# Residuals and means added on VectorE, output blocks turned one layer later, and weight sums stored in whole rows, in a fused routing attention and MLP kernel

## The chip, the cores and the metric

The kernel runs on one core of one Trainium2 chip. The metric is the device time of one execution in microseconds (us). A core has five engines with a queue each: TensorE (PE: matmuls, with weight loads, PEld, beside them), VectorE (DVE), ScalarE (ACT), GpSimd (POOL) and SyncE (SP). Each works through its instructions in order; semaphores tie them together. DMA transfers are issued from SP, ACT or POOL. Here only POOL issues transfers that add to what lies at the destination.

## The reference

```python
# q, k, v: (4, 8, 768, 64), centroids: (8, 16, 64), fp32; w_ch1: (512, 2048), w_ch2: (2048, 512)
mask = q_assign[:, :, :, None] == k_assign[:, :, None, :]     # the same nearest centroid
scores = np.where(mask, scale * np.matmul(q, k.transpose(0, 1, 3, 2)), -1e9)
attn = softmax(scores)
x = np.matmul(attn, v).transpose(0, 2, 1, 3).reshape(4, 768, 512)
xn = (x - mu) / np.sqrt(var + 1e-06) * g_ln                   # mean and variance over the 512
out = x + np.maximum(xn @ w_ch1, 0.0) @ w_ch2                 # fp32
```

## The kernel before, in words

**Stages.** The attention of all four batches comes first: 16 pairs of heads, each in turn. Its results go to DRAM twice, features by positions (`xT_d[b]`) and positions by features (`x_d[b]`). While it runs, the two weight matrices are loaded in chunks (`raw`) and converted; POOL finishes each chunk by a transfer that adds its second half (`w<-tb`, L274). Then come, for batch 0, a first and a second layer, and for batches 1, 2 and 3 each a first layer and a deep layer.

**The first layer** is x times w1 with seven instead of eight products for each pair of 2x2 blocks. It has eight units `j`, each with seven parts (`first_layer(b, j, part)`); parts 4 and 3 of a unit are issued inside the next one. A part is four matmuls with 384 columns (L810). VectorE adds the results (L841), ScalarE copies banks (L836) and applies ReLU (L849). `w1_sums` prepares block sums of w1 on VectorE for the next unit. `unit_end` is the work behind a unit: rows for the next batch's statistics (`norm_rows`), in batch 1 the splitting of w2 (`w2_split`), block sums of the hidden values (`outer_sums`), and from unit 5 on the first loads of the ring.

**The deep layer** is hidden times w2 with two levels of the scheme: seven outer products `m` in the order 4, 7, 1, 6, 5, 2, 3, each made of seven inner ones `way`, so 49 steps (`STEPS`), written here as (m, way). Ways 4 and 3 of a product come behind way 2 of the next. A step (`deep_product`) is four pairs of matmul records with 192 columns (L1084); its weights are a quarter of a block of w2, 256 KB, loaded into a ring of ten slots (`ring_load`), ten steps ahead, on SP. Its hidden operand is a quarter or a sum of quarters: `inner_sums` (L1058, L1060) and `inner_late` (L1065, L1067) make the sums on VectorE. Results are drained by `put_in`: copies by ScalarE (L1097) where nothing is added, additions by VectorE (L1099) where an earlier block is added. After each step `behind(m, way)` puts other work into the queues:

- the last two parts of the first layer and `outer_sums` of its last units at (4, 2), `outer_late` at several steps (L1046);
- `add_rest`: the residual, by accumulating transfers on POOL (L1123), eight per layer;
- `norm_load`, `norm_stats`, `norm_stat_rows`, `norm_center`, `norm_apply`: the next batch's rows are loaded, the mean is added by four accumulating transfers on POOL (L583), the scale is applied by VectorE (L593);
- `sum_onto` (L1164), and one accumulating transfer of block 7 onto block 4 (`m<-m`, L1204);
- `x_sum`, `w1_sums`: sums for the next first layer;
- `turn` (L1135): VectorE transposes a finished output block in 32x32 pieces, and `leave` stores it in eight transfers of 48 KB (L1147), two per step on SP. In the last batch the block of product 3 goes out in four parts (`last_part`, L1173).

**Order and queues.** In the first and deep layers of batches 1 to 3 the orders of TensorE, VectorE, ScalarE and SP are those of the program text. In the attention and in batch 0 SP's order is chosen by the scheduler when the kernel is built. Buffers rotate in pools: `unit` has eight of 128x768, `row` two (rows of statistics), `sums` two.

**Stored weights.** `w2_all` is a copy of w2 in DRAM, stored in four transfers of 1 MB in batch 1's first layer; `w2_t` holds four sums of blocks, `w2_d` the sums of quarters. A ring load from `w2_d` reads 2 KB in a row for each partition, one from `w2_all` or `w2_t` reads four pieces of 512 B.

Of the kernel before, what the change touches and what calls it, by code (L numbers as in the profile page):

```python
# [19 lines left out]
def kernel(  # L20
# [528 lines left out]
    def norm_stats(b, parts=range(2)):  # L549
# [9 lines left out]
        if 1 in parts:  # L559
            stat = moments[b, "stat"]  # L560
            if b == 0:
                nc.vector.tensor_scalar_mul(stat[:, 0, :], mv[:, :, 1], -1.0)
            else:
                nc.vector.tensor_copy(stat[:, 0, :], mv[:, :, 0 if b == 1 else 1])
            nc.vector.reciprocal(stat[:, 1, :], stat[:, 1, :])

    def norm_stat_rows(b):
# [7 lines left out]
        for i in range(2):  # L575
            if i or b < 2:
                row = xpool.tile([P, S], F32, tag="row", name="stat_row", bufs=2)
                nc.sync.dma_start(out=row, in_=stat_d[b][i : i + 1, :].to_broadcast([P, S]))
                moments[b, i] = row

    def norm_center(b):
        for c in range(NDC):
            nc.gpsimd.dma_start(  # L583
                out=normed[b][0][:, c, :], in_=stat_d[b][0:1, :].to_broadcast([P, S]), accum_op=ALU.add
            )
# [299 lines left out]

    def w2_sum(st, i):
        if i in (1, 3):
            st["t", i] = xpool.tile([P, NFH, MH], F32, tag="sums", name=f"w2t{i}", bufs=2)
        elif i == 2:
            st["t", 2] = xpool.tile([P, NFH, MH], F32, tag="sums", name="w2t2", bufs=2)  # L890
        o, x, y = {
            1: lambda: (st["t", 1], w2_block(0, 1), w2_block(0, 0)),
            2: lambda: (st["t", 2], w2_block(1, 1), st["t", 1]),
            3: lambda: (st["t", 3], w2_block(1, 1), w2_block(0, 1)),
            4: lambda: (st["t", 2], w2_block(1, 0), st["t", 2]),
        }[i]()
        for c in range(0, NFH, 2):
            nc.vector.tensor_tensor(o[:, c : c + 2], x[:, c : c + 2], y[:, c : c + 2], ALU.subtract)
# [13 lines left out]
    def second_product(bank, tt, lhs, rhs, first):  # L912
        for c in range(NFH):
            nc.tensor.matmul(  # L914
                bank[:, :MH], hidden[lhs + (c,)][:, tt * P : (tt + 1) * P], rhs[:, c, :],
# [24 lines left out]
    def second_layer(b, tt, part, st):  # L940
        if part == 1:
            st["x", tt] = ps("x_ps")
            second_product(st["x", tt], tt, (0, 0), w2_block(0, 0), True)
            st["p1", tt] = add_rows(b, 0, tt, 0, st["x", tt])
        elif part == 2:
            y = ps("y_ps")
            second_product(y, tt, (0, 1), w2_block(1, 0), True)
# [14 lines left out]
        elif part == 3:  # L962
            second_product(st["z", tt], tt, (0, 1), w2_block(1, 1), False)
# [18 lines left out]
    w2_all = spill.tile([NFC, P, DM], F32, name="w2_all")  # L982
# [3 lines left out]
    def w2_keep(i, t):  # L986

        nc.sync.dma_start(out=w2_t[i - 1], in_=t.rearrange("p c f -> p (c f)"))

    def w2_back(i):  # L990
        t = splits.tile([P, NFH, MH], F32, tag="t", name="w2_t")
        nc.sync.dma_start(out=t.rearrange("p c f -> p (c f)"), in_=w2_t[i - 1])
        return t

    def w2_split(m, src):

        blocks = [[src[:, l * NQH : (l + 1) * NQH, j * P : (j + 1) * P] for j in range(2)] for l in range(2)]
# [9 lines left out]
    def w2_operand(m, way):  # L1007
# [3 lines left out]
        if m in SUMS:  # L1011
            src = w2_t[SUMS.index(m)].rearrange("p (c f) -> p c f", f=MH)
        else:
            r, k = {1: (0, 0), 2: (1, 0), 3: (1, 1)}[m]
            src = w2_all[r * NFH : (r + 1) * NFH, :, k * MH : (k + 1) * MH].rearrange("c p f -> p c f")
        return src[:, l * NQH : (l + 1) * NQH, j * P : (j + 1) * P]
# [31 lines left out]
    def inner_sums(st, m, which):  # L1048

        (a11, a12), (a21, a22) = quarters(m)  # L1050
        if 0 in which:
            if "tmp" not in st:
                st["tmp"] = xpool.tile([P, 3, S], F32, tag="sums", name="qs", bufs=2)
                st["n"] = 0
# [3 lines left out]
            nc.vector.tensor_tensor(s1, a21, a22, ALU.add)  # L1058
# [534 lines left out]
```

## Time and profile before

| what | value |
|---|---|
| median of 3 runs | 936.92 us (936.36 to 942.41) |
| the profiled execution | 935.08 us, span 933.2 us, mean clock 0.984 |
| busy | PE 890.0, PEld 582.4, DVE 683.6, ACT 392.7, POOL 121.1 us |
| DMA | 151.39 MB, mean 162 GB/s; queue q1 (SP) 52.3%, q0 (POOL) 16.2% of 16 engines' span |
| first layer of batch 1, deep layer of batch 1 | 475.0 to 544.4, 544.4 to 629.5 us |
| first layer of batch 2, deep layer of batch 2 | 629.5 to 699.2, 699.2 to 778.3 us |
| first layer of batch 3, deep layer of batch 3 | 778.3 to 847.9, 847.9 to 917.7 us |

A line of the windows view gives a stretch, its length, the busy time of each engine with its number of instructions, the granted TensorE clock (PEclk, 1.00 is full), the mean busy share of the 16 DMA engines and their GB/s. A share a little over 1 comes from transfers that reach over the edge of a stretch. A line of the chain view gives start, length and what the chain of latest releases went through; "DMA m<-xT_d" is a transfer to `m` from `xT_d`. In a timeline the bracket at the end is the idle time ahead of the instruction and what ended it. In the DMA view the last number is the median time from issue to landing.

### The profile page before, as it was taken

What the parts mean: (1) busy time and instruction counts of PE and PEld (TensorE: products, weight loads), DVE (VectorE), ACT (ScalarE), POOL (GpSimd) and SP (SyncE); (2) the same over time, 40 slices, a digit from 0 to 9 for tenths busy, and PEclk for the clock granted to TensorE, in tenths of its full rate; (3) what the DMA queues carried; (4) which work ended last, traced back from release to release, by engine and by line L of the source; (5) the groups of instructions that cost most, each with busy time, mean ns of one, the idle gap of its engine ahead of it and who ended that gap; (6) DMA issues with size and microseconds to landing.
All of it is one profiled execution on the core that took longest, in us unless ns stands there. A gap on an engine that the chain in (4) does not pass through costs nothing.

```text
span 933.2 us, 13290 instructions
## 1 busy us (share of the span) xinstructions
PE 890.0 (95%) x4724; PEld 582.4 (62%) x4724; DVE 683.6 (73%) x1145; ACT 392.7 (42%) x715; POOL 121.1 (13%) x178
## 2 busy tenths in 40 slices
PE   8999999999999999999999988989999799999993
PEld 4444444444444455588865568975558796557992
DVE  6999999998988878985647667664548586447672
ACT  4777768999767723310025521004551001332100
POOL 1122222211212111100000003210002120000220
PEclk9999999999999999999999999899999899999997
DMA  7788899896994457644347779972137996102994
GB/s 155 161 174 159 182 179 199 193 230 130 205 176 96 101 138 172 172 146 155 123 141 283 266 263 211 285 134 58 32 115 196 257 229 138 37 1 67 235 215 80
DMA packets 286440, 151.39 MB, mean 162 GB/s; under 512 B 211856, under 2 KB 251392, under 8 KB 285344
## 3 DMA queue, kind: packets, MB, share of 16 engines
q1 hardware_dynamic: 253728, 125.61, 52.3%
q0 software_dynamic: 28176, 24.13, 16.2%
q10 hardware_dynamic: 4464, 0.74, 0.4%
q8 instruction: 39, 0.64, 0.3%
q14 instruction: 33, 0.27, 0.1%
HBM read 107.61 MB, written 33.25 MB: 151 GB/s over the span
## 4 chain that ended last, share of the span: by engine, by line
PE 55%; DMA 6%; issue 2%; DVE 2%; POOL 0%; SPq 0%; DVEq 0%; POOLq 0%
PE x_ps L810 18%; PE z_ps L810 9%; PE x_ps L1084 8%; PE x_ps L914 4%; PE y_ps L810 4%; PE z_ps L1084 4%; DMA m<-xT_d 2%; PE z_ps L914 2%; DMA w<-w_all 2%; PE y_ps L1084 2%; DMA m<-m 1%; PE y_ps L914 1%; PE s_ps L386 1%; PE a_ps L398 1%; DMA out_dram<-y 1%
## 5 line engine op out<-in xcount | busy, mean ns | idle before, releaser
L381 ACT ACTIVATE e<-s_ps 128x768 f32<-128x768 f32 x192 | 151.7, 812 | 9.1 <-PE s_ps L386 4.9
L386 PE MATMUL s_ps<-t,t 64*128 64x384 f32 x768 | 154.9, 483 | 0.0
L398 PE MATMUL a_ps<-e,v_sb 128*64 128x384 f32 x768 | 130.9, 490 | 0.0
L398 PEld LDWEIGHTS a_ps<-e,v_sb 128*64 128x64 f32 x768 | 52.3, 137 | 75.8 <-issue 62.8
L1084 PE MATMUL x_ps<-lower,w 128*128 128x192 f32 x448 | 84.5, 336 | 12.6 <-issue 5.6
L841 DVE TENSOR_TENSOR lower<-z_ps,u 128x384 f32<-128x384 f32 x56 | 31.1, 556 | 81.7 <-PE z_ps L810 54.6
L386 PEld LDWEIGHTS s_ps<-t,t 64*128 64x128 f32 x768 | 68.2, 188 | 35.1 <-issue 34.2
L1123 POOL DMA_DIRECT2D m<-xT_d x24 | 32.6, 1461 | 440.8 <-ACT m L1097 198.7
L1084 PEld LDWEIGHTS x_ps<-lower,w 128*128 128x128 f32 x448 | 76.0, 195 | 16.9 <-issue 9.3
L836 ACT COPY p<-x_ps 128x384 f32<-128x384 f32 x32 | 15.1, 472 | 137.5 <-PE x_ps L810 137.5
L386 PE MATMUL s_ps<-mask,mask 64*128 64x384 bf16 x384 | 63.0, 324 | 1.1 <-ACT e L381 0.7
L849 ACT ACTIVATE lower<-lower 128x384 f32<-128x384 f32 x88 | 45.2, 522 | 41.8 <-DVE lower L841 41.8
L433 DVE TENSOR_TENSOR two<-e 128x1536 f32<-128x1536 f32 x30 | 52.6, 1753 | 12.6 <-ACT e L381 12.3
L836 ACT COPY u<-x_ps 128x384 f32<-128x384 f32 x64 | 30.7, 479 | 69.8 <-PE x_ps L810 69.8
L436 DVE TENSOR_TENSOR two<-two,e 128x1536 f32<-128x1536 f32 x30 | 52.5, 1750 | 1.7
L810 PE MATMUL x_ps<-xn,w 128*128 128x384 f32 x128 | 46.6, 487 | 0.0
L810 PE MATMUL x_ps<-xn,ws 128*128 128x384 f32 x128 | 46.5, 486 | 0.0
L810 PE MATMUL z_ps<-xn,ws 128*128 128x384 f32 x128 | 46.5, 486 | 0.0
L810 PE MATMUL x_ps<-xt,w 128*128 128x384 f32 x128 | 46.5, 486 | 0.0
L810 PE MATMUL z_ps<-xt,ws 128*128 128x384 f32 x128 | 46.5, 486 | 0.0
L810 PE MATMUL y_ps<-xn,w 128*128 128x384 f32 x128 | 46.5, 486 | 0.0
L810 PE MATMUL x_ps<-xt,ws 128*128 128x384 f32 x128 | 46.5, 486 | 0.0
(212 smaller groups left out, 1499.2 us busy)
## 6 DMA issues: line engine op xcount, KB each, us to landing
w<-w_d SPq DMA_DIRECT2D x84, 256.0 KB, 5.2
raw<-in_moe_w_ch_dram SPq DMA_DIRECT2D x32, 512.0 KB, 4.9
w<-w_t SPq DMA_DIRECT2D x36, 256.0 KB, 6.1
w<-tb POOLq DMA_DIRECT2D x32, 256.0 KB, 6.4
w_d<-wt SPq DMA_DIRECT2D x7, 1024.0 KB, 5.5
w<-w_all SPq DMA_DIRECT2D x27, 256.0 KB, 5.9
v_sb<-in_v_dram SPq DMA_DIRECT2D x32, 192.0 KB, 5.9
xr<-x_d SPq DMA_DIRECT2D x24, 256.0 KB, 3.0
```

The costliest lines, as they stand in the source:

```text
L381: nc.scalar.activation(e, s[:, :, :HC], AF.Exp, scale=SCALE)
L386: nc.tensor.matmul(s[:, j, :HC], of_keys[:, keys], of_queries[:, o : o + HC], start=part == first, stop=part != first, skip_group_check=True,)
L398: nc.tensor.matmul(acc[j * D : (j + 1) * D, :HC], loaded[n]["v"][:, j, c, :], e[:, j, :], start=(c == 0), stop=(c == NT - 1),)
L433: nc.vector.tensor_tensor(two, soft.pop(u), soft.pop(u + 1), ALU.add)
L436: nc.vector.tensor_tensor(two, two, soft.pop(u + 2), ALU.add)
L810: nc.tensor.matmul(bank[:, :HC], lhs[:, c, :], rhs[:, c], start=first and c == 0, stop=c == NDH - 1, skip_group_check=True,)
L836: nc.scalar.copy(t, bank[:, :HC])
L841: nc.vector.tensor_tensor(h, bank[:, :HC], other, ALU.add)
L849: nc.scalar.activation(h, h, AF.Relu)
L914: nc.tensor.matmul(bank[:, :MH], hidden[lhs + (c,)][:, tt * P : (tt + 1) * P], rhs[:, c, :], start=first and c == 0, stop=c == NFH - 1, sk ...
L1084: nc.tensor.matmul(bank, w[:, c, :], a[:, c], start=way in (1, 2, 5) and c == 0, stop=c == NQH - 1, skip_group_check=True,)
L1123: nc.gpsimd.dma_start(out=o[:, h].rearrange("p (t q) -> p t q", t=NT), in_=xT_d[b][2 * j + h].rearrange("p (t q) -> p t q", t=NT)[:, :, r ...
```

## The change

- The residual is loaded into SBUF by two plain transfers per layer on SP (`rest_load`) and added by VectorE (`add_rest`), four times per layer. The mean is subtracted by VectorE (`norm_apply` with `i` = 0), four times. Block 7 is added to block 4 by VectorE. Products 6 and 5 no longer add an earlier block as their banks are drained; whole blocks are added later (`sum_onto`, five per layer, before two).
- Of the four output blocks of batches 1 and 2, one is turned in the deep layer; three are turned behind units 0 and 1 of the next first layer, from a list `pending`, and stored four transfers per unit. The turned blocks lie in the `row` buffers; `unit` has six buffers. In the last batch all are turned earlier, and SP and ACT share the stores.
- `outer_sums`, three quarters of the first `inner_sums`, `norm_stats` and `norm_stat_rows` move from the deep layer into the first layer, parts 4 and 3 of its last unit to (4, 1) and (4, 2).
- `w2_all` and `w2_t` are laid out by quarters, so that every ring load reads 2 KB in a row. `w2_all` is stored in 16 transfers, which the scheduler places on SP in the attention and in batch 0's first and second layer. Split 6 of w2 moves from unit 7 to unit 6.

```diff
     def norm_stat_rows(b):
...
         for i in range(2):
-            if i or b < 2:
-                row = xpool.tile([P, S], F32, tag="row", name="stat_row", bufs=2)
-                nc.sync.dma_start(out=row, in_=stat_d[b][i : i + 1, :].to_broadcast([P, S]))
-                moments[b, i] = row
-
-    def norm_center(b):
-        for c in range(NDC):
-            nc.gpsimd.dma_start(
-                out=normed[b][0][:, c, :], in_=stat_d[b][0:1, :].to_broadcast([P, S]), accum_op=ALU.add
-            )
+            row = xpool.tile([P, S], F32, tag="row", name="stat_row", bufs=2)
+            nc.sync.dma_start(out=row, in_=stat_d[b][i : i + 1, :].to_broadcast([P, S]))
+            moments[b, i] = row
...
-    w2_all = spill.tile([NFC, P, DM], F32, name="w2_all")
+    w2_all = spill.tile([2, 2, 2, 2, P, NQH * P], F32, name="w2_all")
...
+    def w2_whole(back):
+        for r in range(2):
+            for k in range(2):
+                for l in range(2):
+                    for h in range(2):
+                        c, m = r * NFH + l * NQH, k * MH + h * P
+                        w = w2[:, c : c + NQH, m : m + P]
+                        d = w2_all[r, k, l, h].rearrange("p (c f) -> p c f", f=P)
+                        nc.sync.dma_start(out=w if back else d, in_=d if back else w)
...
     def unit(name):
-        return units.tile([P, 2, HC], F32, tag="unit", name=name, bufs=8)
+        return units.tile([P, 2, HC], F32, tag="unit", name=name, bufs=6)
...
-    def add_rest(b, r, j, o):
-        for h in range(2):
-            nc.gpsimd.dma_start(
-                out=o[:, h].rearrange("p (t q) -> p t q", t=NT),
-                in_=xT_d[b][2 * j + h].rearrange("p (t q) -> p t q", t=NT)[
-                    :, :, r * 2 * Q : (r + 1) * 2 * Q
-                ],
-                accum_op=ALU.add,
-            )
+    def rest_load(b, k):
+        if b + 1 == B and k:
+            t = xpool.tile([P, 3, S], F32, tag="sums", name="rest_x", bufs=2)[:, :2]
+        else:
+            t = units.tile([P, 2, S], F32, tag="rest", name="rest_x", bufs=1)
+        nc.sync.dma_start(out=t, in_=xT_d[b][2 * k : 2 * k + 2].rearrange("h p s -> p h s"))
+        rest_x[b, k] = t
+
+    def add_rest(b, r, k, o):
+        o = o.rearrange("p h (t q) -> p h t q", t=NT)
+        x = rest_x[b, k].rearrange("p h (t q) -> p h t q", t=NT)[:, :, :, r * 2 * Q : (r + 1) * 2 * Q]
+        nc.vector.tensor_tensor(o, o, x, ALU.add)
...
-    def turn(b, r, j, o):
-        y = unit("y")
+    def turn(b, r, k, o):
+        y = xpool.tile([P, S], F32, tag="row", name="y", bufs=2)
...
-            onto = {6: 1, 5: 6, 2: 1, 3: 5}.get(m)
+            onto = {2: 1, 3: 5}.get(m)
...
+        def between():
+            first_layer(b, NFH - 1, 3)
+            relu(len(summed))
+            outer_sums(NFH - 1, True)
+            rest_load(b, 0)
+            if more:
+                norm_load(b + 1)
+            else:
+                rest_load(b, 1)
...
+        jobs = {
+            (4, 1): [lambda: first_layer(b, NFH - 1, 4)],
+            (4, 2): [between],
+            (4, 3): [rest(1, 0, 4)],
+            (7, 6): [s4(0)], (7, 4): [s4(1)], (7, 3): [s4(2)], (1, 6): [s4(3)],
+            (1, 4): [onto(4, 7)], (6, 3): [onto(6, 1)],
+            (5, 4): [onto(4, 6)], (5, 3): [onto(5, 6)], (2, 6): [onto(7, 5)],
+        }
...
+        if more:
+            for at, (i, c) in (
+                ((4, 4), (0, 0)), ((7, 5), (0, 1)), ((1, 3), (0, 2)), ((6, 6), (0, 3)),
+                ((6, 5), (1, 0)), ((6, 4), (1, 1)), ((5, 6), (1, 2)), ((5, 5), (1, 3)),
+            ):
+                jobs.setdefault(at, []).append(norm(i, c))
+            jobs[2, 4] = [out_of(1, 0, 4)]
+            jobs[2, 3] = [rest(0, 0, 2), lambda: rest_load(b, 1)]
+            jobs[3, 6] = [lambda: x_sum(b + 1, 1)]
+            jobs[3, 5] = [lambda: w1_sums(b + 1, 0, (0, 1))]
+            jobs[3, 4] = [lambda: x_sum(b + 1, 2)]
+            later(
+                rest(1, 1, 7), out_of(1, 1, 7), out_of(0, 0, 2), None,
+                rest(0, 1, 3), out_of(0, 1, 3), None,
+            )
+        else:
+            jobs[1, 3] = [rest(1, 1, 7)]
+            jobs[5, 6] = [rest(0, 0, 1), onto(4, 6)]
+            del jobs[5, 4]
+            jobs[2, 5].append(rest(0, 1, 5))
+            jobs[2, 1] = [out_of(1, 0, 4)]
+            jobs[2, 7].append(out_of(1, 1, 7))
+            jobs[2, 3] = [out_of(0, 0, 2)]
...
-            leave(2)
+            leave(2 if more else 4, (nc.sync,) if more else (nc.sync, nc.scalar))
...
+            if part == 5 and b and j:
+                outer_sums(j - 1, b > 1 or j > 4)
+                if j + 1 == NFH:
+                    inner_sums(deep[b], ORDER[0], cs=slice(0, NQH - 1))
...
-                m = (1, 5, 3, 4, 2, 7, None, 6)[j]
+                m = (1, 5, 3, 4, 2, 7, 6, None)[j]
...
-            if j > 1:
-                outer_sums(j - 2, b > 1)
+                if j in (5, 6):
+                    outer_late("s", "e", (0, 0), j - 5)
+            while pending:
+                job = pending.pop(0)
+                if job is None:
+                    break
+                job()
+            if b + 1 < B and j + 2 == NFH:
+                norm_stats(b + 1)
+            if b + 1 < B and j + 1 == NFH:
+                norm_stat_rows(b + 1)
+            leave(4)
```

## The prediction

> **What bounds the kernel now.** I read the busy shares first (TensorE, "PE", 890.0 of 933.2 us), then cut the span into stages at the places where TensorE changes from the first layer (L810) to the deep layer (L1084). These are the stretches of the windows view; the columns are length, busy PE, weight loads, DVE (VectorE), ACT (ScalarE), POOL (GpSimd), clock, DMA share, GB/s.
>
> ```profile
> 544.40:629.50 85.10, 72.83 (x402) 69.28 (x401) 61.37 (x101) 5.96 (x18) 14.94 (x13) 0.94 0.95 216
> 699.20:778.30 79.10, 70.84 (x403) 67.46 (x402) 57.12 (x96) 6.08 (x18) 14.98 (x13) 0.96 0.96 212
> 847.90:917.70 69.80, 67.20 (x401) 64.95 (x399) 51.23 (x87) 5.74 (x16) 13.08 (x11) 1.00 0.88 191
> 917.70:933.20 15.50, 0.04 (x1) 0.00 (x0) 0.74 (x2) 0.00 (x0) 0.00 (x0) 0.57 0.23 38
> 629.50:699.20 69.70, 69.70 (x219) 41.08 (x218) 32.71 (x69) 33.52 (x82) 0.00 (x0) 1.00 0.25 69
> 778.30:847.90 69.60, 69.60 (x217) 41.00 (x216) 32.71 (x69) 24.39 (x52) 0.00 (x0) 1.00 0.17 47
> ```
>
> The same deep layer takes 85.1, 79.1 and 69.8 us in batches 1, 2 and 3; behind it comes a tail of 15.5 us without matmuls. The first layers between (the last two lines) are full for TensorE, and there DVE is busy for 47% and DMA for 17 to 25%. A deep step (eight matmul records) takes 1.30 us in the timeline, a first-layer part 1.29, so TensorE's floor for 49 steps and two parts is 66.3 us. The losses are 18.8, 12.8, 3.5 and the tail. The chain of waits names what fills them:
>
> ```profile
> 576.65 10.76 DMA m<-m
> ...
> 598.66 9.52 DMA m<-xT_d
> ...
> 613.32 6.52 DMA m<-xT_d
> ...
> 721.21 17.79 DMA w<-w_all
> ```
>
> First the accumulating POOL transfers that add residuals (`m<-xT_d`) and blocks (`m<-m`), then weight quarters for the ring (`w<-`). TensorE's own timeline shows the second kind:
>
> ```profile
> 577.38 1.46 PE L1084 MATMUL x_ps<-w 128*128 128x192 f32 x8
> 583.06 2.93 PE L1084 MATMUL y_ps<-w 128*128 128x192 f32 x8 [4.22 <-DMA w<-w_t]
> 585.78 2.89 PE L1084 MATMUL x_ps<-lower,w 128*128 128x192 f32 x8
> ```
>
> The weights were late by 4.22 us, and the next two steps ran at twice their time; that is the 0.94 in the clock column. Why late: the DMA view of 721 to 740 us.
>
> ```profile
> q0 software_dynamic: 2012, 2.29, 72.2%
> ...
> w<-w_d SPq DMA_DIRECT2D x6, 256.0 KB, 7.9
> w<-w_t SPq DMA_DIRECT2D x3, 256.0 KB, 12.5
> ```
>
> POOL's queue takes 72% of the engines for 2.29 MB, and weights land in 8 to 12.5 us; at 700 to 712 us, without it, they land in 2.6 and 3.5. The ring covers ten steps, 13 us.
>
> **The change, part by part.**
>
> *POOL's additions leave (batches 1 to 3).* Per layer go 8 `m<-xT_d` (192 KB), 4 `xn<-stat_d` (384 KB, 15.1 us each to land; batches 1, 2) and one `m<-m`. In come two plain loads `rest_x` of 768 KB. DMA demand of a middle layer: 39 ring loads of 256 KB, 10.2 MB; next rows 1.6; `rest_x` 1.6; stores 0.4: 13.8 MB in 66.3 us, 208 GB/s. From 531 to 544 us the trace shows 323 GB/s on plain loads and stores alone. The tightest stretch is the start, where 3.1 MB of rows and residuals come beside the ring: at 323 GB/s a ring load is 9.7 us later, plus 2.6 to land, 12.3 against 13 us of cover. Much of it is issued gradually, so I cost it at nothing; without the cover it costs 1 to 3 us in batches 1 and 2 each.
>
> *VectorE takes them.* Wide operations (128x768; 0.95 us, but issued every 0.87 us in a row, 571.42 to 572.29) in a deep layer of batch 2: before 14+14 inner sums, 4 outer, 4 scalings, 2 block sums, 4 turns, 2 row sums = 44. After: 12+14, 4, 4 scalings and 4 centerings, 5 block sums, 2 residuals, 1 turn, 2 row sums = 48. Reads of a bank (0.36 us, every 0.27): 37 before, 29 after, as products 6 and 5 no longer add an earlier block and their copies go to ACT, 0.32 us each, which is busy for 6 of 79 us. So 48x0.87+29x0.27 = 49.6 us against 48.3: about equal, but in 66 instead of 79 us. The new list gives nearly every step of 1.30 us one wide operation and at most one read (1.14 us); exceptions (two wide ones at steps 5 of products 7, 6, 5) are followed by lighter steps. DVE also waited 3.52 us at 608.28 and 3.36 at 619.93 for `m<-xT_d`; with it went TensorE's waits on `lower L1065` (1.25, 1.09). Next late is the copy `u3` between the last products: 0.45 us stays, as in batch 3.
>
> *Outer sums and the first inner sums move into the first layer.* Each deep layer now starts with 3.60, 2.00 and 2.01 us without matmuls ahead of (4,6): DVE ends L1065 at 553.3, TensorE starts at 553.41. After, DVE has only two short sums (0.3 us each) and L1065 left after the last first-layer add: 1.0+0.5+0.6+1.0 = 3.1 us after the layer's start, and (4,6) is due at 2x1.30+2x1.29 = 5.2. These stalls go. Batch 1's units 5 and 6 get fuller: 3 adds and 4 weight sums (3.2), outer 1.5, splitting 2.6, `outer_late` 0.9 = 8.2 of 9.03 us. The split of sum 6 comes a unit earlier, 9 us after its load is issued; the 1 MB load lands in 7.4. Hidden; else it delays DVE by 1 to 2 us, which unit 7 (no splitting) takes up.
>
> *Whole rows.* 21 ring loads per layer come in 2 KB instead of 512 B rows. The row: 3.5 us for `w_t` in 512 B pieces against 2.6 for `w_d` in 2 KB, in the same quiet 12 us. The Trainium skill, "DMA: Bandwidth & Descriptors", Specifications, says that transfers reach line rate from 512 B on, so this part would bring nothing. By the row it saves 21x0.9 = 19 us of landing per layer, by the rule 0; on TensorE's path both make 0 once POOL's traffic is gone, since either lies within 13 us. I take the row for the cover alone. The 16 stores of `w2_all` move ahead to the attention and batch 0's first layer, in SP's queue before `raw` loads: the first group waits for a weight's addition issued at 352.10 (landing in 6.4: 358.5; next `raw` 361.2), the second to about 381 (next `raw` 381.67). Hidden by 2.7 and 0.7 us; bounds 0 to +6. I take +0.5.
>
> *Three blocks turned later.* Per batch 24 of 32 stores move into the next first layer, four per unit on SP (0.62 us each to issue, 2.8 to land). DVE gets 2 residuals and 3 turns there, 4.5 us in two units with half their time free. **It adds a wait:** the fourth turn reuses the buffer of the second, whose last four stores are issued only in unit 1, in batch 2 behind a row load that waits for ACT's statistics. By durations DVE arrives 17 us after the layer's start, the statistics end at 17.6, four issues 20.5, landing 23.3: DVE stands 6 us. Queued behind it are the adds of unit 2, and the weight sums that unit 3's part 6 needs at 6.45+9.03+9.03+3x1.29 = 28.4 (five, seven, seven and three parts); DVE, with the turn (0.9), two adds (1.0) and the sums (1.5) to do, has them at 26.7. Hidden by 1.7 us; bounds 0 and +5. I take +1.0.
>
> *The tail.* After the last matmul SP is still issuing a backlog:
>
> ```profile
> 921.30 2.41 SPq L1147 DMA_DIRECT2D out_dram<-y  x3
> 923.81 3.85 SPq L1177 DMA_DIRECT2D out_dram<-y  x6
> ```
>
> The last turn ends at 918.55; SP's last issue at 927.66; 5.5 us lie behind it. After, the first two blocks are turned at products (2,1) and (2,7) and SP and ACT share the stores. Of ACT's work only one copy, (5,4), lies behind two of them. What is left is four short stores, two per queue, 1.3 us, and some lag: 0.8+1.3+5.5+0.9 = 8.5 instead of 15.5.
>
> **The sum.** Deep layers to the floor plus 0.75 for the last copies and 1.0 for small lateness of DVE: 68.0, 68.0; batch 3 without row work 67.2. Gains 17.1+11.1+2.6+7.0 = 37.8; costs 0.5+1.0. Net -36.3 from the profiled run's 935.08 (span 933.2 plus 1.9): 898.8, **899 us**. The median of the runs shown, 936.92, is 1.8 higher, well inside the range.
>
> **Rivals.**
> *VectorE becomes the bound.* It would have 75% of the deep layer by issue times, in order, so each wait for ACT or a load is passed on. Against it: batch 3 does 43 us of this work in 69.8 and hardly delays TensorE. Then all three layers stay at 69.8: -15.3-9.3-0, tail -4, first layers +3: 909.5.
> *The ring stays late.* For it: 12.3 against 13 us above. Half of the losses of batches 1 and 2 stay: -15.8, batch 3 -1, tail -3: 915.
> *The stores hold DVE, and the time rises.* The place is unit 1 of batches 2 and 3. TensorE is safe for 7.8 us of DVE's standing (6.1 plus the 1.7 left). Beyond that each us costs one, in two layers; the 37.8 us are used up when the wait reaches 27 us, and at 29 the time is 935.1-37.8+0.5+42.4 = 940. Against it: 24 stores behind the deep layer of batch 1 took 23.33 us of SP (0.97 each), so four take 4.
>
> **How the numbers follow.** Forecast 0.63, VectorE 0.19, late ring 0.10, stores 0.05, better than all costs 0.03. The floors without any cost give 935.1-35.1-7.9 = 892. The range 892 to 917 reaches over the late ring. A measurement of this kernel can tell about 1% from no change: faster by more than that (below 927.6) takes the first three and the last, less some for causes unseen, 0.91; within 1% 0.04; slower 0.05.
>
> **What would show it.** Right: deep layers of 67 to 69 us at a DMA share near 0.7 and clock 1.00; no q0 traffic behind 410 us; ring loads landing in 3 to 5 us; TensorE back to back at (4,6); a tail near 8.5. Wrong: first layers of batches 2 and 3 longer than 69.7 with DVE's turn waiting for `out_dram` (stores); PE waits on `w<-` (ring) or on DVE's L1074 and L1108 lines (VectorE); holes before 400 us with DVE waiting for `raw`.

## The result and the profile after

The changed kernel takes **897.56 us** (median of 4 runs, 896.93 to 900.04) beside 939.26 us (4 runs of the kernel before, 936.36 to 942.41). The ratio is 0.956, with a 95% interval from 0.9517 to 0.9603. The forecast was 899, the range 892 to 917. The profiled execution took 897.76 us, with a span of 896.0.

The windows view, cut at the same places as before. The columns are stretch, length, busy PE, PEld, DVE, ACT and POOL with their numbers of instructions, clock, DMA share, GB/s. The lines are the deep layers of batches 1, 2 and 3, then the tail, then the first layers of batches 2 and 3.

```profile
544.00:614.00 70.00, 67.01 (x402) 65.06 (x401) 58.04 (x89) 8.32 (x25) 0.00 (x0) 1.00 0.75 234
683.70:750.80 67.10, 66.65 (x402) 65.28 (x401) 57.53 (x88) 8.31 (x25) 0.00 (x0) 1.00 0.72 225
820.40:887.50 67.10, 66.65 (x401) 65.06 (x399) 52.47 (x84) 8.17 (x24) 0.00 (x0) 1.00 0.72 197
887.50:896.00 8.50, 0.15 (x1) 0.00 (x0) 0.73 (x2) 0.00 (x0) 0.00 (x0) 0.74 0.23 38
614.00:683.70 69.70, 69.70 (x218) 40.97 (x217) 39.12 (x84) 33.76 (x83) 0.00 (x0) 1.00 0.29 71
750.80:820.40 69.60, 69.60 (x218) 41.05 (x217) 38.94 (x82) 24.39 (x52) 0.00 (x0) 1.00 0.23 56
```

The deep layers went from 85.1, 79.1 and 69.8 us to 70.0, 67.1 and 67.1, at full clock, and the tail from 15.5 to 8.5. The first layers took the three turns and stayed at 69.7. POOL does nothing any more in these stages. The page's DMA issues (number, KB each, median us to landing) show the ring in time:

```profile
w<-w_d SPq DMA_DIRECT2D x84, 256.0 KB, 3.4
w<-w_t SPq DMA_DIRECT2D x36, 256.0 KB, 4.9
w<-w_all SPq DMA_DIRECT2D x27, 256.0 KB, 3.2
```

TensorE's timeline shows the start of the deep layer of batch 1. In the kernel before, (4,6) began 3.60 us late, and the steps behind it took up to 2.77 us:

```profile
548.35 1.45 PE L810 MATMUL z_ps<-xn,ws 128*128 128x384 f32 x4
553.41 1.68 PE L1084 MATMUL x_ps<-lower,w 128*128 128x192 f32 x8 [3.60 <-issue]
554.88 2.77 PE L1084 MATMUL z_ps<-qs,w 128*128 128x192 f32 x8
```

In the changed kernel it is back to back; the last line is the one loss that is new:

```profile
547.91 1.45 PE L803 MATMUL z_ps<-xn,ws 128*128 128x384 f32 x4
549.35 1.54 PE L1093 MATMUL x_ps<-lower,w 128*128 128x192 f32 x8
...
565.13 1.57 PE L1093 MATMUL x_ps<-lower,w 128*128 128x192 f32 x8 [2.54 <-DMA w<-w_all]
```

Where it comes from is seen on SP (same kernel, timeline of SP's queue; the length is that of the issues):

```profile
544.76 0.36 SPq L574 DMA_DIRECT2D stat_d<-st  x1
549.08 0.80 SPq L577 DMA_DIRECT2D stat_row<-stat_d  x2
...
551.94 0.44 SPq L1137 DMA_DIRECT2D rest_x<-xT_d  x1
552.43 3.42 SPq L521 DMA_DIRECT2D xn<-xT_d  x4
556.30 1.46 SPq L1035 DMA_DIRECT2D w<-w_all  x2
```

SP stands from 545.1 to 549.1 for the store of the statistics, because it has to load them back. Then the residual and four row blocks, 2.3 MB, go out in one piece, and the ring load stands behind them. In batch 2 the same list of issues costs nothing; there SP stands for the store for only 1.0 us:

```profile
684.56 0.32 SPq L574 DMA_DIRECT2D stat_d<-st  x1
685.85 0.80 SPq L577 DMA_DIRECT2D stat_row<-stat_d  x2
```

The difference lies ahead of the store: in batch 1 SP had issued 1 MB of split weights (`w_d<-wt`) and four ring loads from 540.8 to 544.5, and the DMA engines were full until 548; in batch 2 it had issued nothing from 676 us on.

### The profile page after: what moved, and what is told of

Read it like the earlier page. It is cut to its first block, busy times and chain, and to the rows that moved or that the text cites. A ratio compares the mean times of both kernels' runs of the same rounds, so it can differ in the third digit from the quotient of the medians.

```text
span 896.0 us, 13278 instructions
## 1 busy us (share of the span) xinstructions
PE 879.3 (98%) x4724; PEld 576.4 (64%) x4724; DVE 701.6 (78%) x1158; ACT 400.1 (45%) x739; POOL 77.9 (9%) x141
## 4 chain that ended last, share of the span: by engine, by line
PE 62%; DMA 2%; DVE 0%; SPq 0%; issue 0%; ACT 0%
PE x_ps L803 18%; PE x_ps L1093 11%; PE z_ps L803 9%; PE z_ps L1093 6%; PE x_ps L910 5%; PE y_ps L803 5%; PE y_ps L1093 3%; PE z_ps L910 2%; PE y_ps L910 1%; PE s_ps L386 1%; DMA w<-w_all 1%; PE a_ps L398 1%; DMA w<-w_d 1%; DMA stat_d<-st 0%; PE den_ps L452 0%; DVE u L1108 0%
## 5 line engine op out<-in xcount | busy, mean ns | idle before, releaser
L1093 PE MATMUL x_ps<-lower,w 128*128 128x192 f32 x448 | 81.2, 327 | 3.4 <-DMA w<-w_all 2.5
L1093 PEld LDWEIGHTS x_ps<-lower,w 128*128 128x128 f32 x448 | 73.9, 190 | 5.7 <-DMA w<-w_all 2.8
L386 PEld LDWEIGHTS <-mask 64*128 64x128 bf16 x384 | 19.2, 94 | 42.3 <-issue 11.3
```

The source lines that it names most:

```text
L386: nc.tensor.matmul(s[:, j, :HC], of_keys[:, keys], of_queries[:, o : o + HC], start=part == first, stop=part != first, skip_group_check=True,)
L1093: nc.tensor.matmul(bank, w[:, c, :], a[:, c], start=way in (1, 2, 5) and c == 0, stop=c == NQH - 1, skip_group_check=True,)
```

## The experiments

Twelve more kernels ran. To compare them I cut each trace at the same places. All lengths are us of one profiled execution each; "start" is where the deep layer of batch 1 begins, "deep 1" to "deep 3" are the deep layers of batches 1 to 3. The times are medians. The kernels ran in three groups, each on a chip of its own, on which the kernel before had 937.3, 938.6 and 939.1 us; the ratios given are to these. A difference of 1 to 2 us between the times of two groups says little; the lengths of the stages say more.

| kernel | time | start | deep 1 | deep 2 | deep 3 | tail |
|---|---|---|---|---|---|---|
| before | 939.3 | 544.5 | 85.1 | 79.1 | 69.8 | 15.5 |
| before, whole rows alone | 936.9 | 544.5 | 84.1 | 80.4 | 71.5 | 14.3 |
| the same, nobody waits for the residual | 928.4 | 543.5 | 78.1 | 82.3 | 71.1 | 13.8 |
| only the order, residual at its old places | 918.8 | 544.2 | 77.4 | 72.7 | 73.6 | 8.8 |
| only the order | 909.3 | 543.5 | 75.2 | 69.9 | 71.7 | 8.0 |
| after, residual and mean by POOL | 907.4 | 544.1 | 72.9 | 69.0 | 71.6 | 8.2 |
| after, mean by POOL | 900.9 | 544.9 | 71.6 | 68.9 | 67.2 | 7.9 |
| after, residual by POOL | 900.2 | 544.1 | 68.1 | 67.0 | 71.6 | 7.9 |
| after, 512 B pieces | 900.0 | 544.0 | 72.2 | 67.1 | 67.2 | 8.2 |
| after, sums back in the deep layer | 904.2 | 543.6 | 70.8 | 70.8 | 69.4 | 8.5 |
| after, all turns in the deep layer, slow stores at the end | 914.7 | 543.9 | 74.3 | 68.9 | 67.2 | 17.5 |
| after, more work for VectorE | 900.5 | 544.1 | 69.7 | 67.1 | 68.5 | 8.3 |
| after, loads spread out | 896.0 | 544.4 | 67.0 | 67.0 | 67.2 | 9.4 |
| after | 897.6 | 544.0 | 70.0 | 67.0 | 67.2 | 8.3 |

### 1. Whole rows, taken away and alone

```diff
-    w2_all = spill.tile([2, 2, 2, 2, P, NQH * P], F32, name="w2_all")
+    w2_all = spill.tile([NFC, P, DM], F32, name="w2_all")
...
+                if j < 4:
+                    cs = slice(j * NFC // 4, (j + 1) * NFC // 4)
+                    nc.sync.dma_start(out=w2_all[cs].rearrange("c p f -> p c f"), in_=w2[:, cs])
```

> The changed kernel with the old layout of w2_all and w2_t (ring loads from them read 512 B pieces) and w2_all stored in batch 1's first layer again. Theory (the accumulating transfers of POOL were the disturbance, short pieces cost only landing time inside the ring's cover): 897 to 900 us, at most 2 us above the changed kernel, all of it at the start of the deep layer of batch 1, where a ring load was late by 2.54 us already. Rival (whole rows bring a good part of the gain): 908 us or more, with waits on w<-w_t and w<-w_all in all three deep layers.

Measured: 899.95 us (899.43 to 900.07; ratio 0.9579, 0.9549 to 0.9608). The loss lies in batch 1's deep layer, 72.2 instead of 70.0; the late ring load is the same one, now with a wait of 3.12 us. Only 0.6 us of the loss is the longer wait; the rest is that the next two steps took 2.52 and 2.24 us, at a granted clock near 0.6. So whole rows are worth about 2 us in this execution, and only where the ring is at its limit. By the times alone it is not certain: one of the four runs of the changed kernel, 900.04 us, was as slow as these.

The other way round, the kernel before with this layout alone:

> The kernel before with the layout by quarters alone (whole rows of 2 KB, w2_all stored in 16 transfers early); the POOL transfers stay. Theory: 934 to 939 us, the waits on w<- in batches 1 and 2 stay, as POOL's queue still holds 72% of the engines at the ring's loads. Rival (whole rows bring a good part): 920 to 928 us, the waits of 4.22 and 17.79 us on w<-w_t and w<-w_all mostly gone.

Measured: 936.88 us (10 runs, 935.31 to 939.23; ratio 0.9989, 0.9971 to 1.0007). No gain that can be measured, and the time is the one that the theory expected. The trace is not: the waits for `w<-`, which were to stay, went. First the waits of TensorE and VectorE in the kernel before, from the waits view (total, times, longest; us); VectorE's from 540 us on:

```profile
PE y_ps L1084 <- DMA w<-w_t: 5.7, 2, 4.2
...
PE x_ps L1084 <- DVE lower L1065: 2.3, 2, 1.3
...
DVE p L1099 <- DMA m<-xT_d: 11.9, 4, 3.5
```

The same rows with whole rows alone:

```profile
PE x_ps L1098 <- DVE lower L1079: 12.4, 3, 6.9
...
PE y_ps L1098 <- DMA w<-w_t: 0.2, 1, 0.2
...
DVE p L1113 <- DMA m<-xT_d: 22.9, 5, 9.1
```

The ring was repaired: TensorE's waits for `w<-` fell from 9.0 us (5.7, 2.0 and 1.3) to 1.3 (0.9, 0.2 and 0.2). The time stayed, since a second wait had been lying underneath. VectorE, draining products 2 and 3 (`p<-x_ps,m`), adds a block onto which POOL is still adding the residual. With the ring on time TensorE arrives earlier, VectorE stands longer, and TensorE stands for VectorE.

### 2. Residual and mean, one by one and together

```diff
     def add_rest(b, r, k, o):
-        nc.vector.tensor_tensor(o, o, x, ALU.add)
+        for h in range(2):
+            nc.gpsimd.dma_start(out=o[:, h]..., in_=xT_d[b][2 * k + h]..., accum_op=ALU.add)
```

("..." inside a line stands for what is left out of it. The plain loads of `rest_load` are not issued either.)

> The changed kernel, but the residual is again added by POOL's accumulating transfers (eight of 192 KB per layer) at the places where VectorE adds it now. Theory: half of the POOL traffic is back, 1.57 MB per layer in all three layers; 903 to 912 us, ring loads landing later, and VectorE standing for m<-xT_d in front of the turn that follows. Rival (what brought the gain is the moved sums and the later turns, and VectorE has no room): 897 to 899 us or a little faster, since VectorE gives up four wide operations per layer.

Measured: 900.17 us (900.01 to 900.36; ratio 0.9583, 0.9554 to 0.9613). That lies between the theory's 903 to 912 and the rival's 897 to 899. In batch 2 nothing is lost (67.0), and batch 1 even gains 1.9 (68.1): without the plain load of the residual at its start the late ring load is late by 0.9 us and not 2.54. All of the loss is in batch 3 (71.6 instead of 67.2), the one batch where the new list adds the residual onto block 1 at (5,6), a few steps before the drain of product 2 reads that block. The timelines of VectorE and, below, of TensorE in batch 3:

```profile
869.58 0.36 DVE L1108 TENSOR_TENSOR p<-x_ps,m 128x192 f32<-128x192 f32 x1 [3.60 <-PE z_ps L1093]
...
881.01 0.36 DVE L1108 TENSOR_TENSOR p<-x_ps,m 128x192 f32<-128x192 f32 x1 [1.90 <-DMA m<-xT_d]
```

```profile
870.86 1.57 PE L1093 MATMUL x_ps<-lower,w 128*128 128x192 f32 x8 [1.29 <-DVE lower L1074]
...
882.29 1.57 PE L1093 MATMUL x_ps<-lower,w 128*128 128x192 f32 x8 [0.51 <-DVE lower L1074]
```

The first bracket names a matmul on `z_ps`, but the drain reads `x_ps` and `m`, and POOL had issued its two transfers to `m` at 862.55, which land in a median of 6.0 us in this stretch: of several waits the row names one, and here the transfer is the one that fits.

The mean alone:

```diff
                 norm_load(b + 1)
+                norm_center(b + 1)
...
-                ((4, 4), (0, 0)), ((7, 5), (0, 1)), ((1, 3), (0, 2)), ((6, 6), (0, 3)),
```

`norm_center` is four transfers of 384 KB that add the mean, on POOL.

> The changed kernel, but the mean is again added by four accumulating transfers of 384 KB on POOL, issued right behind the loads of the next rows, in batches 1 and 2 only. Theory: these fall on the tightest stretch, 3 to 18 us behind the start of the deep layer; the ring is late by 3 to 8 us in each of the two layers, 904 to 914 us, batch 3 unchanged at 67.1. Rival (the gain is from the moved sums and later turns): 897 to 899 us.

Measured: 900.94 us (900.72 to 901.55; ratio 0.959, 0.956 to 0.9619): 1.6 and 1.9 us in the deep layers of batches 1 and 2, as ring waits of 0.6 to 1.1 us each. The mechanism is the expected one, the size is below the expected 3 to 8.

Both together:

> The changed kernel with residual and mean both added by POOL's accumulating transfers again; whole rows, moved sums and later turns stay. Alone the residual cost 2.6 us and the mean 3.4. Theory A (contention: the transfers together starve the ring, as the prediction had it): much more than the sum, 915 to 925 us, with ring waits of 10 us and more in each of the deep layers of batches 1 and 2. Theory B (the transfers hurt before because a drain on VectorE waited for them, which the new order of additions has taken away): about the sum, 902 to 907 us.

Measured: 907.36 us (905.71 to 908.05; ratio 0.9676, 0.9634 to 0.9717), 9.8 above the changed kernel, where the two alone make 6.0. The excess is in batch 1. POOL issues the first residual among the mean's four transfers, its second half behind all four, at about 562 us; it lands some 20 us later, and VectorE's block sum waits for it:

```profile
585.48 0.96 DVE L1186 TENSOR_TENSOR m<-m,m 128x768 f32<-128x768 f32 x1 [9.83 <-DMA m<-xT_d]
```

Contention (theory A) would have given 915 or more; the order (theory B), 902 to 907, is nearer.

### 3. The order alone

The changed kernel with three of its contents undone: residual and mean by POOL, 512 B pieces, the old time of storing. What stays is where and when everything is done: the sums moved into the first layer, the later turns, the list of additions, the two queues for the last stores. Block 7 onto block 4 stays with VectorE too.

> The changed kernel with all three transfers' parts undone: residual and mean by POOL, weights in 512 B pieces, w2_all stored in batch 1's first layer. What is left of the change is the order: sums moved into the first layer, whole blocks added later, three blocks turned later, stores on two queues in the last batch. Theory A (contention): the ring is late as in the kernel before, 918 to 928 us. Theory B (order): 904 to 911 us, since pieces alone cost 2.4 us and the two additions alone 2.6 and 3.4.

Measured: 909.30 us (907.68 to 911.93; ratio 0.9702, 0.9657 to 0.9747). Its deep layers and tail in the windows view:

```profile
543.50:618.70 75.20, 69.64 (x402) 66.68 (x401) 52.99 (x83) 8.34 (x25) 11.88 (x11) 0.98 0.94 229
688.50:758.40 69.90, 67.57 (x403) 65.10 (x402) 52.33 (x82) 8.34 (x25) 11.90 (x11) 1.00 0.95 228
828.00:899.70 71.70, 67.83 (x401) 64.95 (x399) 49.01 (x79) 8.19 (x24) 10.61 (x8) 1.00 0.86 185
899.70:907.70 8.00, 0.00 (x0) 0.00 (x0) 0.74 (x2) 0.00 (x0) 0.00 (x0) 0.77 0.21 37
```

POOL's transfers are all there but one (`m<-m`) and the DMA share is 0.94 and 0.95, as before the change. Yet the deep layers of batches 1 and 2 take 145.1 us together and not 164.2. **Of the 27 us gained in these two stages, 19 come from the order, with block 7's addition, and 8 from what else VectorE and the layout took over.** The ring is a part of the 8: TensorE waits for `w<-` for 6.9 us in this kernel, 9.0 before and 2.5 after the change. Batch 3 gains nothing from the order (71.7, before 69.8).

Is it the waiting for transfers, or the moved sums and turns? The same kernel, with POOL's residual put back to where it was issued before:

```diff
-            (4, 3): [rest(1, 0, 4)],
+            (7, 6): [s4(0), rest(1, 0, 4)],
-            (1, 4): [onto(4, 7)], (6, 3): [onto(6, 1)],
+            (1, 4): [onto(4, 7), rest(1, 1, 7)], (6, 3): [onto(6, 1), rest(0, 0, 1)],
-            (5, 4): [onto(4, 6)], (5, 3): [onto(5, 6)], (2, 6): [onto(7, 5)],
+            (5, 4): [onto(4, 6)], (5, 3): [onto(5, 6), onto(7, 5), rest(0, 1, 5)],
```

In batch 3 of this kernel block 4 is turned before block 6 is added to it, so that part of the sum is missing there; the instructions are the same in number.

> The kernel with only the order of the change (909.3 us measured: residual and mean by POOL, 512 B pieces), with POOL's residual transfers put back to where the kernel before issued them: onto block 4 at (7,6), onto 7 at (1,4), onto 1 at (6,3) and onto 5 at (5,3), whose blocks the drains of products 2 and 3 add soon after. Theory B (what held the kernel before was a drain or a block sum on VectorE that waits for a transfer): 915 to 925 us, VectorE waiting for m<-xT_d in each deep layer and TensorE for VectorE behind it. Rival (it was the moved sums and the later turns): 908 to 911 us.

Measured: 918.78 us (915.69 to 920.29; ratio 0.9774, 0.9735 to 0.9812), 9.5 above "only the order". Each deep layer is longer by 1.9 to 2.8 us, in batch 3 with the same eight transfers of residuals in it, and VectorE stands as the expectation said; from its timeline, batches 1, 2 and 3:

```profile
601.95 0.36 DVE L1105 TENSOR_TENSOR p<-x_ps,m 128x192 f32<-128x192 f32 x1 [2.67 <-DMA m<-xT_d]
...
744.46 0.36 DVE L1105 TENSOR_TENSOR p<-x_ps,m 128x192 f32<-128x192 f32 x1 [3.07 <-DMA m<-xT_d]
...
885.05 0.36 DVE L1105 TENSOR_TENSOR p<-x_ps,m 128x192 f32<-128x192 f32 x1 [3.97 <-DMA m<-xT_d]
```

So the waits for the residual are 5.0 of the 19 us in batches 1 and 2. Undone one by one in the changed kernel (experiments 4 and 5 below), the moved sums cost 4.6 us in these two stages and the later turns 6.2. That makes 15.8, a rough sum, since waits cover one another; what is left, and the share of block 7's addition, was not separated.

The waits from the other side. In the kernel before with whole rows, the residual's transfers go to a spare buffer that nobody reads, so the residual is left out of the result:

```diff
     def add_rest(b, r, j, o):
+        if b not in spare:
+            spare[b] = xpool.tile([P, S], F32, tag="row", name="spare", bufs=2)
+            nc.gpsimd.memset(spare[b], 0.0)
...
+        o = spare[b]
```

> The kernel before with whole rows (936.9 us measured), its residual transfers kept in number, size and place, but added to a spare buffer that nobody reads, so the residual is left out of the result. The traffic stays and VectorE's wait for m<-xT_d goes. Theory A (contention): 933 to 937 us. Theory B (VectorE's drain waits for the transfer, TensorE for VectorE): the 12.4 us that TensorE waits for DVE lower go, 922 to 927 us, with what is left in the start stalls of 7.6 us, the tail of 15.5 and some ring waits.

Measured: 928.37 us (5 runs, 925.73 to 930.35; ratio 0.9893, 0.9857 to 0.9929), 8.5 below whole rows alone and just above theory B's 922 to 927. In the profiled run the gain is in batch 1 (78.1 instead of 84.1), with 1.0 at the start; batch 2 even rose, from 80.4 to 82.3. TensorE's waits, and VectorE's timeline in batches 1 and 2:

```profile
PE x_ps L1098 <- DVE u L1113: 13.8, 6, 8.7
PE x_ps L1098 <- issue: 7.6, 3, 3.6
```

```profile
589.65 1.02 DVE L593 SCALAR_TENSOR_TENSOR xn<-xn,g_sb,stat_row 128x768 f32<-128x768 f32 x1 [4.89 <-DMA xn<-stat_d]
...
747.19 0.96 DVE L1185 TENSOR_TENSOR m<-m,m 128x768 f32<-128x768 f32 x1 [8.00 <-DMA m<-m]
```

The wait for `m<-xT_d` went and others appeared under it. VectorE stands for the mean's transfer (`xn<-stat_d`, 4.89 us here and 4.04 in batch 2), and in batch 2 for 8.00 us for block 7's addition onto block 4 (`m<-m`); behind that one TensorE stands for the 8.7 us of the first line. So before the change the ring, the residual, the mean and block 7 lay on top of one another, all of them held by transfers that share one set of engines. Taking away one shows the next.

### 4. The sums at the start

```diff
-            if part == 5 and b and j:
-                outer_sums(j - 1, b > 1 or j > 4)
-                if j + 1 == NFH:
-                    inner_sums(deep[b], ORDER[0], cs=slice(0, NQH - 1))
...
+            outer_sums(NFH - 2, True)
+            inner_sums(deep[b], ORDER[0])
```

> The changed kernel with outer_sums one unit later and the first inner_sums wholly in the deep layer again, as before the change. The stalls of 3.6, 2.0 and 2.0 us ahead of (4,6) were measured before. If they come back whole: 905 us. If they were only what stood in front of other waits: 897 to 900 us. They may also pay back 2.5 us, as the ring load that was late in batch 1 gets time: then 902 to 903 us.

Measured: 904.16 us (903.13 to 905.21; ratio 0.9644, 0.9603 to 0.9685), 6.6 above. TensorE stands 1.9 to 2.0 us in each batch; in batches 1 and 2 the steps behind run slower (2.07 and 2.69 us instead of 1.46), in batch 3 not. From its timeline, batches 2 and 3:

```profile
691.39 2.69 PE L1093 MATMUL x_ps<-fifth,w 128*128 128x192 f32 x8 [1.90 <-issue]
...
831.98 1.54 PE L1093 MATMUL x_ps<-lower,w 128*128 128x192 f32 x8 [2.00 <-issue]
```

In batch 1 the ring load is then no longer late, and only 0.8 us are lost; in batches 2 and 3 it is 3.8 and 2.2.

### 5. Turns and stores

All four blocks turned in the deep layer, by the last batch's list; in batch 3 two stores per step, on SP alone.

```diff
-            later(
-                rest(1, 1, 7), out_of(1, 1, 7), out_of(0, 0, 2), None,
-                rest(0, 1, 3), out_of(0, 1, 3), None,
-            )
...
-            leave(2 if more else 4, (nc.sync,) if more else (nc.sync, nc.scalar))
+            leave(4 if more else 2)
```

> The changed kernel with all four blocks turned and stored inside the deep layer in batches 1 and 2 (the second residual is loaded at the start of the layer), and in batch 3 two stores per step on SP alone. The stages keep the two apart. Deep layers of batches 1 and 2: VectorE gets 2 residuals and 3 turns more, 4.5 us in some 67 of which it is busy for 57.5. Theory (there was room for this, later turns bring little): deep layers of 70 to 72 and 67 to 69 us. Rival (turning later is a main part of the gain): over 73 and 71. Batch 3's tail: 8.3 us now, 15.5 before; if the second queue brought it, 11 to 14 us; if the earlier turns did, 8 to 9.5.

Measured: 914.74 us (913.02 to 915.51; ratio 0.9736, 0.9703 to 0.9769). The windows view of the deep layers of batches 1 and 2 and of the tail, then TensorE's wait in batch 1, then SP at the end:

```profile
543.90:618.20 74.30, 69.51 (x403) 67.56 (x402) 60.70 (x93) 8.31 (x25) 0.00 (x0) 0.95 0.75 228
687.90:756.80 68.90, 67.09 (x402) 65.14 (x401) 60.29 (x92) 8.31 (x25) 0.00 (x0) 1.00 0.73 227
...
893.70:911.20 17.50, 0.00 (x0) 0.00 (x0) 0.73 (x2) 0.00 (x0) 0.00 (x0) 0.65 0.27 44
```

```profile
566.41 2.93 PE L1093 MATMUL x_ps<-lower,w 128*128 128x192 f32 x8 [4.20 <-DMA w<-w_all]
```

```profile
889.94 11.12 SPq L1163 DMA_DIRECT2D out_dram<-y  x10
```

VectorE has room for the turns: TensorE waits for it 1.3 us in all, as in the changed kernel. What costs 4.3 and 1.9 us is that the second residual must then be loaded at the start of the layer, 768 KB more in the tightest stretch: the late ring load of batch 1 is late by 4.20 us and not 2.54, and the two steps behind it run at little over half the clock (2.93 and 2.57 us). So turning later pays through the load that it lets come later, and neither expectation fits both layers: batch 1 is over 73 us, as the rival had it, batch 2 in the theory's 67 to 69. The tail grows to 17.5 us, beyond either expectation, although the blocks are turned as early as in the changed kernel: four stores per step on two queues bring the 8.3, not the earlier turns alone. Rate and queue were changed together here, so which of the two it is stays open.

### 6. Is VectorE near its bound?

```diff
-            nc.vector.tensor_tensor(s1[:, cs], a21[:, cs], a22[:, cs], ALU.add)
+            for _ in range(2 if m != ORDER[0] else 1):
+                nc.vector.tensor_tensor(s1[:, cs], a21[:, cs], a22[:, cs], ALU.add)
```

> The changed kernel with the first inner sum of six products per deep layer computed twice: six wide operations more on VectorE, 5.2 us per layer by 0.87 each, at steps that already had one or two. If VectorE has room: 897.5 to 902 us. If it is all but the bound, each of them shows: 913 us. Partly: one step of 1.30 us holds one wide operation and a read, so a third one at steps 5 of products 7, 6 and 5 may stand 0.5 to 1 us each, 902 to 906 us.

Measured: 900.50 us (898.96 to 902.26; ratio 0.9588, 0.9554 to 0.9622). In batches 1 and 2 the stages stay as long as they were, batch 3 loses 1.3. In batch 2 VectorE is now busy for 62.17 of 67.10 us and TensorE still for 66.65:

```profile
683.70:750.80 67.10, 66.65 (x402) 65.14 (x401) 62.17 (x94) 8.33 (x25) 0.00 (x0) 1.00 0.70 224
```

VectorE was not the bound: in batch 2 it had at least the 4.6 us of room that it was given here.

### 7. A version with the loads spread out

```diff
-                norm_load(b + 1)
+                norm_load(b + 1, (0,))
...
+            for c, at in ((1, (4, 7)), (2, (7, 2)), (3, (7, 6))):
+                jobs.setdefault(at, []).append(lambda c=c: norm_load(b + 1, (c,)))
...
+        queue = nc.gpsimd if b > 1 else nc.sync
+        queue.dma_start(out=stat_d[b].rearrange("s (t p) -> (s t) p", p=P), in_=st)
...
-            leave(4)
+            leave(8)
...
+                queue = nc.gpsimd if way == 4 and i > 1 else (nc.scalar, nc.sync)[i % 2]
```

> The changed kernel with the next batch's four row loads issued at (4,2), (4,7), (7,2) and (7,6) and not all at (4,2), the statistics of batches 2 and 3 stored and loaded through POOL's queue so that SP does not stand behind them, eight stores per unit behind units 0 and 1, and two of the last eight stores on POOL's queue. The late ring load of batch 1 (2.54 us) should go, VectorE's wait of 4.73 us for out_dram too without any effect on the time, and the tail should fall by 0.5 to 1: 893 to 895.5 us. If the ring load was late for another reason: 897 us.

Measured: 895.95 us (5 runs, 895.46 to 896.25; ratio 0.9532, 0.9504 to 0.956). The runs of the changed kernel, 896.93 to 900.04, all lie above these, but they were made on another occasion; the difference of 1.6 us is small beside the intervals. The stage itself is clear:

```profile
544.40:611.40 67.00, 66.55 (x403) 65.18 (x402) 57.86 (x89) 8.33 (x25) 1.66 (x3) 1.00 0.79 244
...
885.00:894.40 9.40, 0.00 (x0) 0.00 (x0) 0.73 (x2) 0.00 (x0) 0.89 (x2) 0.77 0.20 32
```

The late ring load is gone, and batch 1 takes what batch 2 takes; whether the spreading or POOL's queue did it was not separated. VectorE's wait of 4.73 us in unit 1 of batch 2 (next section) fell to 0.73, and the first layer kept its 69.7: that wait cost nothing. The tail got 1.1 us longer with two of the last stores on POOL, against the expectation; which would explain why the time stays just above the expected 893 to 895.5. Without that edit this version should be about 1 us faster, by the length of the tail; that was not run.

## Why the prediction was right, and where it was not

**The sum.** 898.8 forecast for the profiled execution, 897.76 measured. By stages: 68.0, 68.0 and 67.2 forecast for the deep layers, 70.0, 67.1 and 67.1 measured; tail 8.5 and 8.5; costs elsewhere 1.5 forecast, none seen. That these agree to 1 us is in part luck: batch 1 came out 2.0 us over its forecast, batch 2 0.9 under it, and the 1.5 us of costs did not come.

**The two deep layers (17.1 and 11.1 us forecast, 15.1 and 12.0 measured): the size held, the reason only partly.** The prediction read the ring's late loads (4.22 us and the slow steps behind it) as the main loss, put down to POOL's 72% share of the engines, and sized TensorE's waits on VectorE at 1.25 and 1.09 us, because that is what the trace of before showed. That step was mis-sized. Whole rows alone repaired the ring and the time did not move: underneath lay 12.4 us of TensorE waiting for VectorE, which waited for POOL's residual. The order alone, at a DMA share of 0.94, gives 19 of the 27 us. Of its parts the prediction credited the moved sums, and priced the later turns at a cost of 1.0; the order of additions it mentioned in one sentence, as fewer reads of a bank, where the runs show that it took away a dependence of the drains on transfers, worth 5.0 us in these two layers. The total came out because the change removes all the layers of waits, whichever stood on top; it does not vouch for the split.

**Whole rows: 0 forecast, 0 alone and about 2 us inside the change.** The prediction said that either landing time lies within the ring's cover once POOL's traffic is gone. In batches 2 and 3 that holds (67.1 and 67.2 with pieces). In batch 1 it does not. The prediction set a row against a rule of the Trainium skill. In the stretch from 570 to 610 us, which no POOL transfer crowds, `w<-w_t` landed in 3.3 us with pieces of 512 B and 4.0 with whole rows, so nothing is lost there, as "DMA: Bandwidth & Descriptors", Specifications, says. In the crowded one from 550 to 625 us of the kernel before `w<-w_t` landed in 12.8 us, and in 6.3 with whole rows alone; but `w<-w_all`, whose rows changed as well, landed in 6.6 and 7.1. So that the length of the rows made the difference is not shown.

**Start stalls (7.6 us of the deep layers' gain): right in the main.** With the sums back, the three layers lose 6.8 us together, 5.8 of it by standing. Batch 1's stall came back as 1.89 us and not as 3.60.

**The ring's cover, costed at nothing, with 1 to 3 us in batches 1 and 2 each without it: this is the term that failed,** by 2.54 us of waiting, in batch 1 alone. The estimate compared 12.3 with 13 us of transfer time. It counted 3.1 MB at the start, where 2.3 are issued, left out that SP stands 4 us for the statistics first, and put the demand of a layer at 208 GB/s, where the stages show 225 and 234.

**VectorE's standing in unit 1 of batch 2 (+1.0): the wait is there, at 4.73 us and not 6, and costs 0.**

```profile
636.80 0.98 DVE L1149 STREAM_TRANSPOSE y<-m 128x768 f32<-128x768 f32 x1 [4.73 <-DMA out_dram<-y]
```

It lies inside the 7.8 us of room, as worked out, so the +1.0 was too much. The stores of `w2_all` (+0.5) cost nothing either: the deep layer of batch 1 starts at 544.0 and before at 544.5.

**The tail (7.0 us): right,** through stores that leave as fast as the blocks are turned.

**The rivals.** VectorE as the bound (909.5) is refuted by six added operations per layer that cost nothing in two of three layers. The late ring (915) is what remains of it: one load. Stores that hold VectorE (940): 4.73 us of standing where 27 would have been needed.

## What to carry to other kernels

A wait that ends last covers the waits behind it: before crediting a change with the stall that the trace shows, ask what each engine would wait for if it arrived earlier, and look at the engine that passes the wait on. An addition by transfer is cheap where nobody reads the block soon, and dear where an in-order engine's next instruction reads it; putting it where the next drains read it made "only the order" 9.5 us slower with the same bytes. A queue that must wait for its own store before it can load is a poor one to feed TensorE from: with that pair on another queue and the loads spread out, batch 1's deep layer went from 70.0 to 67.0 us.

## What the runs showed of the hardware

While SP stood for `stat_d`, the DMA engines ran dry for 1.3 us (548.5 to 549.8) although 2.3 MB of loads were due. From 556 to 566 us they then moved 398 GB/s, above the 323 on which the estimate rested. SP could load the statistics back 4.3 us after it had issued their store of 6 KB; in batch 2, with nothing issued ahead of it, after 1.3 us.

A wait of TensorE can cost more than its length, because the steps behind it can run at half the clock. Its length alone does not tell whether they do. After 2.54 us of standing (changed kernel) the granted clock stayed at 1.00. After 4.20 us (turns in the deep layer) it was 0.50 for the next step, after 3.12 us (512 B pieces) 0.60, and after 3.60 us (kernel before) 0.90 for the next step and 0.50 for the one behind. But with the sums back in the deep layer (experiment 4) it was 0.54 in the 2.7 us behind a wait of 1.90 us, and 1.00 behind one of 2.00. The Trainium skill, "TensorE: Matmul & The Clock Gate", Part 1, puts the half clock behind at least one idle window of about 3.4 us and calls the window free-running. Equal waits that cost differently agree with the second; half the clock behind 1.90 us does not agree with the first. What decides it is not shown here.
